# Attention scores: the low part of the keys in both partition halves, the third product over all rows, the value products of a step in one run, four prepared blocks

## The chip, the core and the metric

One NeuronCore of a Trainium2 chip runs the whole kernel. The metric is the device time in microseconds (us); the kernel before was run three times. The engines are TensorE (PE; its weight loads are listed apart as PEld), VectorE (DVE), ScalarE (ACT), GpSimd (POOL) and the DMA queue of SyncE (SP).

## What is computed

```python
def _attn_ref(q, k, v, w1, b1, w2):          # B 2, H 8, S 576, D 64
    scores = scale * np.matmul(q, k.transpose(0, 1, 3, 2))
    rel = (pos[:, None] - pos[None, :]).astype(np.float32)
    psi_rel = np.log1p(np.abs(rel))
    psi_i = np.log1p(np.maximum(pos[:, None].astype(np.float32), 1.0))
    x = (psi_rel / psi_i)[..., None]
    bias = np.maximum(x @ w1 + b1, 0.0) @ w2
    scores = scores + bias.transpose(2, 0, 1)[None, :, :, :]
    scores = scores - np.max(scores, axis=-1, keepdims=True)
    attn = np.exp(scores)
    attn = attn / (np.sum(attn, axis=-1, keepdims=True) + 1e-09)
    return np.matmul(attn, v)

def reference(...):
    x = attention output as 1152 rows of 512
    x = _moe_ref(x, ...)      # eight experts, 512 -> 1024 -> 512, with balanced weights P
    return _moe2_ref(x, ...)  # 512 -> 2048 -> 512 with an ELU between
```

## The kernel before

The program has an attention stage (to about 214 us) and, behind it, the expert and feed-forward stage with the products of lines 530 and 717, whose order a planner (`Plan.order`) makes at build time. The change lies in the attention stage, which is ordered by hand: every engine works off its instructions in the order in which the program issues them.

**Blocks and steps.** A block is a pair of heads `hp` and a batch `b`; there are eight. A step is one block and one query tile `t` of 128 rows (64 for `t` = 4): 40 steps. The first four blocks are interleaved (steps 0 to 19, the 64-row tile first), blocks 4 and 5 fill steps 20 to 29, blocks 6 and 7 steps 30 to 39; in these the two 64-row steps come last (28, 29 and 38, 39).

**Precision in two parts.** `load_qk` loads each block's queries and keys, transposed, twice: 64 head dimensions in partitions 0 to 63 and again in 64 to 127. `prep` (line 1152) casts both to fp32r on VectorE (`qs`, `kh`, line 1159), then subtracts on GpSimd: `qs` becomes the high part in one partition half and the low part in the other (line 1164), and `kl` the low part of the keys (line 1165). It is a generator of four pieces: cast, cast, subtractions of head 0, subtractions of head 1. `emit_qk` (line 1184) multiplies: over all 128 rows, (high + low query) times high key (line 1198), four products, two heads by two halves of the keys; then over the 64 rows of the high query, high query times low key (line 1203), four products, two of which can stand side by side in the array, as they use different rows. `QB` is the number of prepared blocks that have room at once.

**A step.** `run_step(s)` goes through the letters of `ORD_A` while bias groups are left (steps 0 to about 12), and of `ORD_B` after that. R, S: score plus bias and minimum of head 0, 1 on VectorE (`emit_ttr`). T, U: transposes of the previous step's exponentials, copied out by ScalarE (T) and VectorE (U). V: the last transpose, copied by ScalarE. N: reciprocal of the sums on VectorE and its broadcast on GpSimd (line 1239). E, F: exponentials on ScalarE. a: one of five pieces of the value products of two steps back (lines 1282, 1285; the fifth piece ends with the transpose of the broadcast reciprocal, line 1295). X: their result is taken out. Q: score products of the next step. p: one piece of `prep`, then two pieces of the background list `bg`. M, O, H, L: the bias network and its loads.

`PS` lists [block, step]: before that step the block's `prep` is put into the queue that p works off. `w_split` (steps 27 and 28) puts six entries into `bg`: four sums on GpSimd (line 302), four times a high part on ScalarE and a low part on VectorE (lines 315, 316), and a load; the third and fourth part need the sums. `ops_first` (steps 35 and 37) does the like for the first operands of the next stage (lines 332, 352, 353).

```python
    for i, s0 in PS:
        if s == s0:
            prep_q.append(prep(i))
    run_step(s)
    ...
    if s == 27:
        w_split()
    if s == 28:
        w_split()
```

## Time and profile before

| | |
|---|---|
| median of 3 runs | 1208.87 us (1208.53 to 1208.88) |
| the profiled execution's own time | 1207.91 us |
| its span, first to last instruction | 1206.1 us |
| PE busy | 1170.9 us, 97% of the span |
| DVE, ACT, POOL busy | 916.1, 626.4, 92.9 us |
| mean granted PE clock | 0.995 |

Busy shares are averages over stages with different limits, and matmuls overlap, so a busy PE is not a PE at its peak. The chain of waits says what released each piece of work; where it stays on PE, PE itself sets the pace. The rows come from one execution; its span and what lies around it make its time. In rows of products and transposes the first operand shape is rows by columns of the array.

### The profile page before, as it was taken

How to read it: one execution, taken by the hardware profiler on the slowest of the kernel's cores; microseconds unless marked ns; L12 is line 12 of the kernel's file. 1: busy time of each engine (PE TensorE's matmuls, PEld its weight loads, DVE VectorE, ACT ScalarE, POOL GpSimd, SP SyncE). 2: the span in 40 equal slices, each digit the busy share in tenths (PEclk: the TensorE clock that was granted, in tenths of full speed). 3: DMA queues.
4: the chain of work that ended last, by engine and by line, in shares of the span. 5: the costliest groups of instructions: out<-in, count | busy, mean ns of one | idle time of the engine just before them, and what ended most of it. 6: DMA issues, size and time to landing. Idle time of an engine off the chain costs nothing.

```text
span 1206.1 us, 19661 instructions
## 1 busy us (share of the span) xinstructions
PE 1170.9 (97%) x7432; PEld 986.9 (82%) x7432; DVE 916.1 (76%) x1932; ACT 626.4 (52%) x1413; POOL 92.9 (8%) x107
## 2 busy tenths in 40 slices
PE   7899999999999999999999999999999988999998
PEld 3467777788888888888888888888888876788887
DVE  8987787664587778778788787787776468788875
ACT  6797667554333444443434444444434346777763
POOL 4402453000000000000000000000000001000000
PEclk9999999899999999999999999999999999999999
DMA  8767741111112233242232323232411101111102
GB/s 227 221 213 200 208 122 35 33 56 53 36 36 79 80 88 102 67 129 76 92 106 88 105 87 104 90 100 68 130 45 53 53 1 36 53 53 36 36 1 79
DMA packets 36285, 104.78 MB, mean 87 GB/s; under 512 B 4064, under 2 KB 4192, under 8 KB 36192
## 3 DMA queue, kind: packets, MB, share of 16 engines
q1 hardware_dynamic: 36192, 103.54, 28.5%
q8 instruction: 58, 0.95, 0.3%
q14 instruction: 35, 0.29, 0.1%
HBM read 81.88 MB, written 21.64 MB: 86 GB/s over the span
## 4 chain that ended last, share of the span: by engine, by line
PE 91%; DVE 3%; ACT 1%; POOL 1%; issue 0%; DMA 0%; ACTq 0%; DVEq 0%
PE y L717 41%; PE m L530 38%; PE av L1285 3%; PE tr L1254 2%; PE bps L1406 2%; PE sc L1198 1%; PE sc L1203 1%; PE av L1295 1%; PE trl L1266 1%; PE av L1282 1%; PE lg L873 0%; DVE ol L353 0%; DVE et L1213 0%; DVE w1l L316 0%; DVE ol L430 0%
## 5 line engine op out<-in xcount | busy, mean ns | idle before, releaser
L530 PE MATMUL m<-oh,w1h 128*128 128x256 f32 (+1 forms) x1120 | 335.8, 300 | 3.8 <-DVE c L562 1.4
L530 PE MATMUL m<-oh,w1l 128*128 128x256 f32 (+1 forms) x1120 | 330.6, 295 | 3.8 <-ACT u L543 1.6
L530 PE MATMUL m<-ol,w1h 128*128 128x256 f32 (+1 forms) x1120 | 330.3, 295 | 2.6 <-DVE c L562 1.3
L717 PE MATMUL y<-w2h,hh 128*128 128x512 f32 x720 | 284.6, 395 | 2.9 <-ACT hh L637 1.5
L717 PE MATMUL y<-w2h,hl 128*128 128x512 f32 x720 | 283.4, 394 | 0.0
L717 PE MATMUL y<-w2l,hh 128*128 128x512 f32 x720 | 282.5, 392 | 0.8 <-DVE w2l L430 0.8
L530 PEld LDWEIGHTS m<-oh,w1h 128*128 128x128 f32 x1120 | 211.0, 188 | 45.8 <-ACT u L543 13.3
L530 PEld LDWEIGHTS m<-ol,w1h 128*128 128x128 f32 x1120 | 211.4, 189 | 22.4 <-DVE c L562 1.9
L530 PEld LDWEIGHTS m<-oh,w1l 128*128 128x128 f32 x1120 | 211.3, 189 | 5.6 <-ACT u L543 2.3
L717 PEld LDWEIGHTS y<-w2h,hh 128*128 128x128 f32 x720 | 135.1, 188 | 18.8 <-ACT hh L637 2.3
L717 PEld LDWEIGHTS y<-w2h,hl 128*128 128x128 f32 x720 | 135.1, 188 | 17.8
L543 ACT ACTIVATE p<-m 128x256 f32<-128x256 f32 (+1 forms) x160 | 65.8, 411 | 161.3 <-PE m L530 157.3
L717 PEld LDWEIGHTS y<-w2l,hh 128*128 128x128 f32 x720 | 135.2, 188 | 16.2 <-DVE w2l L430 1.4
L543 ACT ACTIVATE u<-m 128x256 f32<-128x256 f32 (+1 forms) x160 | 65.9, 412 | 132.0 <-PE m L530 128.7
L593 ACT ACTIVATE hh<-c 128x512 fp32r<-128x512 f32 (+3 forms) x128 | 72.1, 563 | 109.7 <-DVE c L562 109.6
L748 DVE SCALAR_TENSOR_TENSOR acc<-y,P,acc 128x512 f32<-128x512 f32 x126 | 94.5, 750 | 37.3 <-PE y L717 35.4
L596 DVE SCALAR_TENSOR_TENSOR hl<-c,hh 128x512 fp32r<-128x512 f32 (+3 forms) x128 | 77.5, 605 | 20.4 <-ACT hh L593 18.6
L562 DVE TENSOR_TENSOR c<-m,u 128x256 f32<-128x256 f32 (+1 forms) x80 | 36.6, 458 | 73.7 <-PE m L530 72.0
L1213 DVE CUSTOM_DVE_ANT_0 et<-sc,bt 128x576 f32<-128x576 f32 (+1 forms) x80 | 57.9, 751 | 22.0 <-PE sc L1203 17.3
L332 POOL TENSOR_TENSOR st<-xt,st 128x256 f32<-128x256 f32 (+1 forms) x8 | 6.7, 835 | 755.2 <-DVE st L332 755.0
L1228 ACT ACTIVATE et<-et,nmx 128x576 f32<-128x576 f32 (+1 forms) x80 | 61.3, 771 | 3.2 <-DVE nmx L1213 3.1
L423 ACT ACTIVATE w2h<-raw 128x512 fp32r<-128x512 f32 x80 | 48.6, 625 | 21.7 <-PE y L717 12.4
(136 smaller groups left out, 1600.1 us busy)
## 6 DMA issues: line engine op xcount, KB each, us to landing
raw<-w1p SPq DMA_DIRECT2D x32, 512.0 KB, 3.6
raw<-w2p SPq DMA_DIRECT2D x32, 512.0 KB, 3.6
scr<-o SPq DMA_DIRECT2D x36, 295.5 KB, 3.5
bt<-scr SPq DMA_DIRECT2D x16, 576.0 KB, 4.9
cw<-w1d SPq DMA_DIRECT2D x16, 512.0 KB, 4.4
wsc<-ca SPq DMA_DIRECT2D x32, 256.0 KB, 4.4
cw<-w2d SPq DMA_DIRECT2D x16, 512.0 KB, 4.4
raw<-wsc SPq DMA_DIRECT2D x16, 512.0 KB, 3.6
```

The costliest lines, as they stand in the source:

```text
L423: act.activation(out=dst(bh.get()), in_=src(), func=ACTF.Copy)
L530: lambda e, w=w, o=o, j=j, k=k: pe.matmul(x["ap"](bank), w.get()[:, ai, j, :], o.get()[:, bi, j, :], start=(k == 0 and i in (1, 2, 5)), st ...
L543: lambda e: act.activation(out=b.get()[:, 0:N], in_=x["ap"](bank), func=ACTF.Copy),
L562: lambda e: eng[e].tensor_tensor(out=blk(b.get()[:, half * N:half * N + N], rev), in0=ap(p), in1=ap(q), op=ALU.add),
L593: op([("A", cA(w))], lambda e: act.activation(out=hh(), in_=ap(), func=ACTF.Relu), r=sk, w=wh, after=gate_)
L596: lambda e: dve.scalar_tensor_tensor(out=bl.get()[:, d], in0=ap(), scalar=0.0, in1=hhf(), op0=ALU.max, op1=ALU.subtract),
L717: lambda e, a=a, w=w, f=f, i=i, y=y, c=c: pe.matmul(y.get(), a.get()[:, c], w.get(), start=(f == 0 and i == 0), stop=(f == 3 and i == 2)),
L748: lambda e: dve.scalar_tensor_tensor(out=a.get(), in0=y.get(), scalar=P[0][:, n, e_:e_ + 1], in1=a.get(), op0=ALU.mult, op1=ALU.add),
L1213: dve.tensor_tensor_reduce(out=e.rearrange("p (x j) -> p x j", x=2), in0=sc[0:r, :, 0:HALF], in1=biast[hp, t][0:r, h].rearrange("p (x j) - ...
L1228: act.activation(out=e, in_=e, func=ACTF.Exp, scale=-1.0, bias=nmx[0:r, h:h + 1], accum_out=sm[0:r, h:h + 1])
L1254: pe.transpose(p[:, 128 * j:128 * j + r], et[0:r, c0:c0 + 128], ident[0:r, 0:r])
L1285: pe.matmul(p[64 * h:64 * h + 64, 0:r], vt[:, j - 1, 64 * h:64 * h + 64], a[:, 4 * h + j - 1, 0:r], start=False, stop=(j == 4), skip_group ...
```

## The change

The low part of the keys, `kl`, is made for both heads in both partition halves (twice the room; each of its subtractions covers 128 partitions instead of 64). The low-key products then run over all 128 rows with the same weights as the first ones, (high + low query) times low key, and each head's four products follow each other. The fifth value piece moves from behind Q to the others, so that the five run as one. `QB` falls from 5 to 4, and `PS` moves four blocks to later steps.

```diff
--- before.py
+++ after.py
@@ -30,7 +30,7 @@
 NB = 2
 LAG = 1
 TO = [4, 0, 1, 2, 3]
-QB = 5
+QB = 4
 AB = 2
 BD = 1
 PRE = 12
@@ -39,9 +39,9 @@
 LV = [1, 2, 3, 4, 20, 19, 32, 28]
 ACC = [2.6, 3.1]
 WARM = 8
-PS = [[3, 0], [4, 12], [5, 16], [6, 19], [7, 25]]
+PS = [[3, 0], [4, 16], [5, 17], [6, 20], [7, 27]]
 ORD_A = "RXTSMOHUapaEaaNpFaLMOVQH"
-ORD_B = "RTSNUXaafLEafappFVQa"
+ORD_B = "RTSNUXaafLEafaappFVQ"
 TOFF = [0, 128, 256, 384, 512]
 TROW = [128, 128, 128, 128, 64]
 NN = [256, 320]
@@ -1152,7 +1152,7 @@
         def prep(i):
             qs = qkp.tile([128, 2, S], F32R, tag="qs", name="qs")
             kh = qkp.tile([128, 2, S], F32R, tag="kh", name="kh")
-            kl = qkp.tile([128, S], F32R, tag="kl", name="kl")
+            kl = qkp.tile([128, 2, S], F32R, tag="kl", name="kl")
             prepped[blocks[i]] = qs, kh, kl
             qr, kr = loaded.pop(i)
             for dst, src in ((qs, qr), (kh, kr)):
@@ -1160,9 +1160,9 @@
                 load["d"] += 0.73
                 yield
             for h in range(2):
-                o, u = slice(64 - 64 * h, 128 - 64 * h), slice(64 * h, 64 * h + 64)
+                o = slice(64 - 64 * h, 128 - 64 * h)
                 pool.tensor_tensor(out=qs[o, h], in0=qr[o, h], in1=qs.bitcast(F32)[o, h], op=ALU.subtract)
-                pool.tensor_tensor(out=kl[u], in0=kr[u, h], in1=kh.bitcast(F32)[u, h], op=ALU.subtract)
+                pool.tensor_tensor(out=kl[:, h], in0=kr[:, h], in1=kh.bitcast(F32)[:, h], op=ALU.subtract)
                 yield
 
         def prep_next():
@@ -1193,14 +1193,10 @@
             sc = [psA("sc") for _ in range(2)]
             qc = slice(TOFF[t], TOFF[t] + r)
             for h in range(2):
-                for x in range(2):
-                    kc = slice(HALF * x, HALF * x + HALF)
-                    pe.matmul(sc[h][0:r, x, 0:HALF], qs[:, h, qc], kh[:, h, kc], start=True, stop=False)
-            for x in range(2):
-                for h in range(2):
-                    kc = slice(HALF * x, HALF * x + HALF)
-                    hs = slice(64 * h, 64 * h + 64)
-                    pe.matmul(sc[h][0:r, x, 0:HALF], qs[hs, h, qc], kl[hs, kc], start=False, stop=True)
+                for w, last in ((kh, False), (kl, True)):
+                    for x in range(2):
+                        kc = slice(HALF * x, HALF * x + HALF)
+                        pe.matmul(sc[h][0:r, x, 0:HALF], qs[:, h, qc], w[:, h, kc], start=not last, stop=last)
             for h in range(2):
                 scs[s, h] = sc[h]
```

## Rows read from the trace of the kernel before

**Rows 1.** The page's chain that ended last, by engine, whole program
```profile
PE 91%; DVE 3%; ACT 1%; POOL 1%; issue 0%; DMA 0%; ACTq 0%; DVEq 0%
```

**Rows 2.** Chain of waits, one ordinary step (start, us, what)
```profile
127.18 0.26 PE trl L1266
127.44 0.54 PE sc L1198 x4
127.97 0.46 PE sc L1203 x3
128.43 0.37 PE av L1285 x4
128.80 0.26 PE av L1295
129.06 0.87 PE tr L1254 x8
129.94 0.22 PE av L1282 x2
130.16 0.81 PE av L1285 x12
```

**Rows 3.** Chain of waits in the steps with bias work
```profile
47.78 2.34 POOL qs L1164
...
101.32 0.59 PE tr L1254 x4
...
103.81 1.02 PE av L1285 x16
```

**Rows 4.** Timeline of VectorE, casts and reductions (start, us, instructions)
```profile
121.74 0.75 DVE L1213 CUSTOM_DVE_ANT_0 et<-sc,bt 128x576 f32<-128x576 f32 x1
...
131.27 0.75 DVE L1159 CAST qs<-ring 128x1152 fp32r<-128x1152 f32 x1
...
132.61 0.75 DVE L1213 CUSTOM_DVE_ANT_0 et<-sc,bt 128x576 f32<-128x576 f32 x1
```

**Rows 5.** Timeline of GpSimd, steps 17, 28 and 29
```profile
124.47 1.42 POOL L1164 TENSOR_TENSOR qs<-ring,qs 64x576 fp32r<-64x576 f32 x1
...
128.86 1.42 POOL L1165 TENSOR_TENSOR kl<-ring,kh 64x576 fp32r<-64x576 f32 x1
...
164.77 0.74 POOL L302 TENSOR_TENSOR st<-raw 128x256 f32<-128x256 f32 x1
165.59 0.73 POOL L302 TENSOR_TENSOR st<-st,raw 128x256 f32<-128x256 f32 x1
...
171.77 1.11 POOL L302 TENSOR_TENSOR st<-raw 128x256 f32<-128x256 f32 x1 [0.74 <-DVE w1l L316]
```

**Rows 6.** Timeline of TensorE, transposes of steps 28, 29 and 31
```profile
162.92 1.04 PE L1254 MATMUL tr<-csb,et 128*128 128x128 f32 x8
...
167.96 0.46 PE L1254 MATMUL tr<-csb,et 64*128 64x64 f32 x4 [0.76 <-ACT aT L1267]
...
176.94 0.66 PE L1254 MATMUL tr<-csb,et 128*128 128x128 f32 x4 [0.77 <-ACT aT L1267]
```

**Rows 7.** Timeline of ScalarE, a part of the second weight split
```profile
175.39 0.63 ACT L315 ACTIVATE w1h<-st 128x512 fp32r<-128x512 f32 x1 [0.69 <-POOL st L302]
```

**Rows 8.** Groups of GpSimd by form, the reciprocal's broadcast
```profile
L1239 POOL TENSOR_TENSOR rcb<-ones,rc 128x128 f32<-128x128 f32 x32 | 13.4, 421 | 92.9 <-DVE rc L1237 73.7 <-PE bps L1406 5.0 <-PE av L1295 4.6
...
L1239 POOL TENSOR_TENSOR rcb<-ones,rc 64x128 f32<-64x128 f32 x8 | 3.7, 464 | 21.0 <-DVE rc L1237 16.7 <-PE bps L1406 3.7 <-PE av L1285 0.5
```

**Rows 9.** Sums by window: span, engines' busy time, PEclk, DMA share, GB/s
```profile
33.10:36.50 3.40, 1.20 (x9) 0.18 (x6) 3.40 (x10) 2.29 (x6) 2.85 (x2) 1.00 0.94 231
36.52:39.93 3.41, 3.41 (x14) 1.23 (x14) 1.93 (x5) 1.02 (x3) 0.00 (x0) 0.50 0.73 263
```

**Rows 10.** Chain of waits behind step 36
```profile
197.89 2.04 DVE ol L353 x2
199.93 0.67 DVE et L1213
```

## What the change will do to the time

> **What bounds the kernel now.** I read the page first, for the chain that ended last: 91% of the span on TensorE (PE) [rows 1]. The change touches only the attention stage (to about 214 us), so I then read the chain of waits there, step by step. In the twenty-odd steps after the bias work has run out (steps 13 to 39, ordered by ORD_B), an ordinary step is eight pieces of PE work that add up to 3.79 us with no wait between them [rows 2]; 3.79 is also the distance from one step to the next. So here a saved PE microsecond is a saved microsecond, until another engine comes last. That happens in three places: at step 3 (Pool's subtractions), in steps 29 and 31, and from step 36 on. At steps 29 and 31 PE waits for the head-1 transposes (line 1254): the exponential of head 1 stands on ScalarE behind the third piece of a weight split, and that piece waits for Pool's sums [rows 6, 7]. From step 36 VectorE's low parts (line 353) run straight into the score reduction [rows 10].
>
> **The score products and the value run (PE).** Removed: the row-split products, .46 us with the change into that form, and the value run of four behind them, .37. Added: four full-row products at the price of the first four (.54/4 = .135 each), .54. Merged: the runs of 12 and 4 cost .81 + .37 = 1.18 [rows 2]; the run of 16 in the earlier steps costs 1.02 [rows 3]. The single transpose that now follows another full-array piece instead of a split one costs an eighth of .87, .11, instead of .26. New step: .87 + .22 + 1.02 + .26 + .11 + 8 x .135 = 3.56. It saves .23. The dearer bound for the four products is their present piece plus the same again for the lost pairing; the cheaper is .46 unchanged; I take .135 since it is the same shape, stream and tile form.
>
> The row shows .46 for four paired products, hardly less than .54 for four full ones. The Trainium skill, "TensorE: Matmul & The Clock Gate", Part 3 on packing small matmuls, says products on different row groups run side by side, which speaks against this change: two pairs would cost two products, .27, and the change would add .27 a step. "TensorEngine Tiling (Array Packing)", Key Properties, says that changing the tiling form drains the engine, which speaks for it. The trace agrees with both: pairs overlap, but the change of form eats most of it.
>
> In steps 4 to 12 (ORD_A) the value run is whole already. There only the products change: +.08 for them, and the four transposes behind them fall from .59 [rows 3] to half of .87, -.155 [rows 2]. That is -.075 each for eight steps, -.6. In the first four steps the query tile has 64 rows and there is little to win behind the products; with a tenth lost there I take -.5 for the stage, between 0 and -.8. Score head 0 is ready after four products instead of seven, head 1 after eight; VectorE starts at nearly the same place, which is off the path, so nothing.
>
> **The preparation (line 1152).** Two casts on VectorE, four subtractions on Pool, two a step. One subtraction of 64 x 576 takes 1.42, four in a row 5.8 (124.47 to 130.28) [rows 5]. Over 128 partitions instead of 64 the kl subtraction might cost more. Pool's broadcast takes .42 on 128 partitions and .46 on 64 [rows 8], so partitions do not count. The dearer bound is the line through .42 at 128 elements and .73 at 256 [rows 5, 8], which gives 1.5 at 576; the cheaper is 1.42, which I take.
>
> With four buffers block 4 can be cast only after step 15, and the list PS moves the others later: block 5 from steps 16 and 17 to 18 and 19; block 7 from 25 and 26 to 27 and 28. Block 6 (20, 21) keeps its distance. This is what costs.
>
> *Block 5.* Its four subtractions are issued in step 19, and the scores of step 21 need them at the end of step 20. Pool works in order and has the broadcast of that step (line 1239) ahead, which waits for the reciprocal, which stands behind the two reductions, which stand behind the casts. From the first reduction to the first subtraction it was 2.73 us (121.74 to 124.47) [rows 4, 5]. Casts start 2.2 after the transposes (131.27 against 129.06) and the next reduction 3.55 after them [rows 2, 4], which with a step of 3.56 is the very start of step 19. So the subtractions run from 2.4 to 2.7 after it to 8.2 to 8.5. The seventh product of those scores (head 1, kl) is due at 3.56 + 2.48 + .81 = 6.85. PE waits 1.5 us (1.0 to 1.9); nothing is behind it that could hide that. Before, block 5 had three steps to spare, so no wait.
>
> *Block 7.* In step 28 the first weight split is also fed: ORD_B calls the preparation, then two background pieces, at each p. Pool's queue was broadcast, four sums; it becomes broadcast, two subtractions, four sums, two subtractions, broadcast, and in step 29 the second four sums. Counted from the transposes of step 28 (162.92) [rows 6]: subtractions start at 2.6 and take 2 x 1.46 (to 5.5), the first two sums 1.55 (164.77 to 166.32) to 7.1, and from there to the released transposes it is 1.64 as before (to 167.96): 8.7 instead of 5.04 [rows 5, 6]. Going on in Pool's queue: all four sums 3.6 (to 9.1), two subtractions (12.1), broadcast (12.5), four sums 3.62 as from 171.77 to 175.39 (16.1), then 1.55 to the transposes of step 31 (176.94): 17.7 instead of 14.02 [rows 5 to 7]. The second contains the first. It costs 3.6 (2.9 to 4.2), and the savings of steps 28 to 30 are swallowed in it. Queued behind the waiting piece on ScalarE are the exponential of head 1 and the copy that frees the transposes' bank; PE waits for that copy.
>
> **Late steps.** Steps 31 to 35 save 4.5 x .23 = 1.0. From step 36 the chain runs through VectorE at its own pace: what PE saves there it waits for [rows 10]; about .1 is left in the tail.
>
> **Sum**, against the profiled execution of 1207.91 (span 1206.1): -.5 - 15 x .23 (steps 13 to 27) + 1.5 + 3.6 - 1.0 - .1 = +.05. That execution is 1 us below the median of the runs, 1208.87; the sum carries over, 1208.9. A measurement of this kernel can tell about .2%, 2.4 us, from no change.
>
> **Rivals.**
> *Gains survive* (25%). If Pool gets to the subtractions as soon as the casts are done, not behind the broadcast, they start 2.4 earlier: the 1.5 is gone and the 3.6 shrinks to 1.2, sum -3.9, 1205.0; with no pile-up at all -5.1, and -6 with the larger early saving, 1203. For it: the casts are done before the step begins, so the order alone holds Pool. Against: the subtraction did start right behind the broadcast [rows 5], and N stands ahead of p in both orders.
> *Pool slowed by VectorE* (22%), slower. A subtraction took 2.34 instead of 1.42 at 47.78 [rows 3], and sums of one shape took .73 and 1.11 [rows 5]. In step 28 Pool's longer queue runs beside VectorE's low parts of the same split. Two to four of its entries at the dearer price add 1.8 to 3.6: 1211 to 1212.5. It decides once the excess of the queue passes the 2.4 us margin of the measurement, i.e. from three such entries on; below that it lies in my own range.
> *The change of form stays* (5%), slower. If only .27 of the split products' .46 is theirs (two pairs at the price of two products) and the .19 left is paid in any case by the next change of form, a step of ORD_B saves .04, not .23: 19.5 steps lose 3.7, the nine of ORD_A 1.7, and the time is 1214.3. Against it: changes of form are fewer after it, and the transposes behind a split run cost .59 where those in a whole run of eight cost .435 [rows 2, 3]. This is what the rule on packing above would give.
> A fall of PE's clock is part of my range, not a rival: after a stretch in which PE was busy 1.20 of 3.40 us the granted clock was .50, the 1.2 GHz level, for 3.41 us [rows 9]. The wait at step 29 could do the same; but PE has 6.1 us of work up to the transposes of step 31 (8.7 to 14.8), due at 17.7, so the 1.7 us that one such stretch costs is hidden there, and .6 of two.
>
> **Numbers.** Forecast (within 1206.5 to 1211.3, no change) 48%; faster than that 25%; slower 27%. The likeliest one's own range is 1207 to 1211; to hold 8 in 10 it reaches to 1203.8 on the side of the surviving gains and 1212.7 on that of the slowed Pool.
>
> **What would show it.** Right: ordinary steps 3.55 apart; a wait of PE for Pool's kl at about the 21st step's scores; a gap of some 4 us before the head-1 transposes of step 29, released by ScalarE behind Pool's sums; the end of attention within 2 us of 214. Wrong: no such gap (Pool's order is not what I think), or ordinary steps still at 3.7 (the change of form was not the cost), or subtractions at twice their price.

## The result and the profile after

Six runs of the changed kernel took 1216.30 us in the median (1214.64 to 1220.36), six of the kernel before on the same chip 1208.45 (1205.47 to 1208.88): 1.0075 times the time, 95% interval 1.0056 to 1.0093. The profiled execution of the changed kernel took 1215.84, its span 1214.0, 7.8 us more than the span of before. The prediction was 1208.9, range 1203.8 to 1212.7: the change is slower, and outside the range.

The chain of waits of the changed kernel, one ordinary step (start, us, what), answers to [rows 2]:

```profile
141.94 1.07 PE sc L1199 x8
143.01 0.87 PE tr L1250 x8
143.88 0.22 PE av L1278 x2
144.10 1.02 PE av L1281 x16
145.13 0.26 PE av L1291
145.39 0.11 PE trl L1262
```

They add up to 3.55 us; before it was 3.79. So the saving is there, to the hundredth, and it is lost somewhere else. Five of the waits of the changed kernel from 104 to 185 us (who waited for whom, us in total, times, longest) name the places:

```profile
DVE et L1209 <- DMA bt<-scr: 5.3, 2, 2.7
...
ACT w1h L315 <- POOL st L302: 4.2, 1, 4.2
...
PE av L1291 <- POOL rcb L1235: 1.5, 1, 1.5
...
PE sc L1199 <- POOL kl L1165: 1.4, 1, 1.4
PE sc L1199 <- POOL qs L1164: 1.2, 1, 1.2
```

The starts of the first score product of each step, laid side by side, cut the loss into stretches. Here and below, "step 19" as a length is the distance from the first score product of step 19 to that of step 20.

| stretch | before | after | difference | predicted |
|---|---|---|---|---|
| steps 0 to 12 | 73.32 | 71.80 | -1.5 | -.5 |
| steps 13 to 18 | 22.23 | 22.85 | +.6 | -1.4 |
| step 19 | 3.79 | 5.12 | +1.3 | -.2 |
| step 21 | 3.79 | 6.72 | +2.9 | +1.3 |
| steps 20, 22 to 27 | 26.51 | 24.88 | -1.6 | -1.6 |
| steps 28 to 31 | 17.01 | 21.80 | +4.8 | +3.6 |
| steps 32 to 35 | 15.14 | 14.22 | -.9 | -1.0 |
| step 36 to the first product of line 530 | 20.63 | 21.81 | +1.2 | -.1 |
| from there to the end | 992.09 | 993.11 | +1.0 | 0 |

**Steps 13 to 18.** VectorE's timeline of the changed kernel (start, us, instructions, in brackets the idle time before and who ended it):

```profile
117.51 0.76 DVE L1209 CUSTOM_DVE_ANT_0 et<-sc,bt 128x576 f32<-128x576 f32 x1 [2.69 <-DMA bt<-scr]
```

and the same view of the kernel before:

```profile
117.91 0.76 DVE L1213 CUSTOM_DVE_ANT_0 et<-sc,bt 128x576 f32<-128x576 f32 x1 [1.60 <-DMA bt<-scr]
```

A load of bias tiles lands at about the same time in both. Before, VectorE waited 1.60 for it and PE none; in the changed kernel VectorE is there earlier and waits 2.69, and the rest reaches PE: steps 15 to 18 take 3.85, 3.92, 4.14 and 3.83, 1.5 us over four steps of 3.55. The shorter steps are only a part of the cause. VectorE's 1.5 us of lead (it stood ready at 114.82 instead of 116.31) are the lead of steps 0 to 12, as steps 13 to 15 took 10.95 against 10.88. And the load took longer: from its issue to VectorE's start 11.6 us (105.96 to 117.51), before 10.2 (107.70 to 117.91); the load of tiles ahead of it 6.5 (102.90 to 109.44), before 5.7 (104.42 to 110.09). In e7_hold, whose program is the changed kernel's up to step 28, they took 9.9 (105.80 to 115.66) and 5.3 (102.74 to 108.02), and steps 15 to 18 took 14.2, with no loss. VectorE's timeline of that run:

```profile
115.66 0.76 DVE L1209 CUSTOM_DVE_ANT_0 et<-sc,bt 128x576 f32<-128x576 f32 x1 [1.57 <-DMA bt<-scr]
```

With steps of 3.79, e2_ps lost .95 where the later load took 11.6, and e12_hold .2 where it took 10.8; e17_sumsfirst, with steps of 3.55, lost .8 at 10.8. By these executions an estimated .6 of the 1.5 come from the shorter steps and the rest from the loads.

**Steps 19 and 21.** PE's timeline, the three products at which it stood:

```profile
131.23 0.33 PE L1291 MATMUL av<-csb,rcb 128*128 128x128 f32 x1 [1.51 <-POOL rcb L1235]
...
136.97 0.53 PE L1199 MATMUL sc<-kh,qs 128*128 128x288 f32 x2 [1.22 <-POOL qs L1164]
...
138.91 0.54 PE L1199 MATMUL sc<-kl,qs 128*128 128x288 f32 x2 [1.42 <-POOL kl L1165]
```

GpSimd's timeline in the same stretch answers to [rows 5]:

```profile
126.97 1.94 POOL L1164 TENSOR_TENSOR qs<-ring,qs 64x576 fp32r<-64x576 f32 x1
128.88 1.94 POOL L1165 TENSOR_TENSOR kl<-ring,kh 128x576 fp32r<-128x576 f32 x1
130.77 0.40 POOL L1235 TENSOR_TENSOR rcb<-ones,rc 128x128 f32<-128x128 f32 x1
...
132.09 1.43 POOL L1164 TENSOR_TENSOR qs<-ring,qs 64x576 fp32r<-64x576 f32 x1
133.60 1.45 POOL L1165 TENSOR_TENSOR kl<-ring,kh 128x576 fp32r<-128x576 f32 x1
135.00 1.92 POOL L1164 TENSOR_TENSOR qs<-ring,qs 64x576 fp32r<-64x576 f32 x1
136.88 1.98 POOL L1165 TENSOR_TENSOR kl<-ring,kh 128x576 fp32r<-128x576 f32 x1
```

and VectorE's casts beside it:

```profile
134.72 0.94 DVE L1159 CAST qs<-ring 128x1152 fp32r<-128x1152 f32 x1
135.59 1.99 DVE L1159 CAST kh<-ring 128x1152 fp32r<-128x1152 f32 x1
```

At 130.77 the broadcast that PE waits for in step 19 comes out from behind block 4's subtractions, the last two of which took 1.94 each beside block 5's casts. The four subtractions of block 5 follow from 132.09. Two of them run alone, 1.43 and 1.45; two run beside block 6's casts, 1.92 and 1.98, and the casts take .94 and 1.99 instead of .75.

**Steps 28 to 31.** PE's timeline, the head-1 transposes of step 29 (they answer to the second line of [rows 6]):

```profile
173.03 0.69 PE L1250 MATMUL tr<-csb,et 64*128 64x64 f32 x4 [4.77 <-ACT aT L1263]
```

GpSimd's timeline up to it:

```profile
166.50 1.43 POOL L1164 TENSOR_TENSOR qs<-ring,qs 64x576 fp32r<-64x576 f32 x1
168.01 1.73 POOL L1165 TENSOR_TENSOR kl<-ring,kh 128x576 fp32r<-128x576 f32 x1
169.70 0.90 POOL L302 TENSOR_TENSOR st<-raw 128x256 f32<-128x256 f32 x1
170.68 0.72 POOL L302 TENSOR_TENSOR st<-st,raw 128x256 f32<-128x256 f32 x1
```

and ScalarE's:

```profile
171.43 0.63 ACT L315 ACTIVATE w1h<-st 128x512 fp32r<-128x512 f32 x1 [4.23 <-POOL st L302]
171.97 0.76 ACT L1224 ACTIVATE et<-et,nmx 64x576 f32<-64x576 f32 x1
...
172.72 0.25 ACT L1263 ACTIVATE aT<-trl 128x128 f32<-128x128 f32 x1
```

The three timelines, read back from PE, are as the prediction has it: transposes behind the copy of the last transpose, that behind the exponential of head 1, that behind a piece of the weight split, that behind GpSimd's sums, these behind two subtractions. And two stretches at half clock, by windows (after the stretch: its length, busy time and instructions of PE, PEld, VectorE, ScalarE and GpSimd, PEclk, DMA share, GB/s):

```profile
171.90:178.70 6.80, 5.67 (x31) 4.66 (x32) 6.14 (x12) 4.40 (x13) 5.70 (x7) 0.50 0.55 161
...
216.30:226.50 10.20, 9.66 (x63) 8.42 (x64) 4.38 (x14) 2.59 (x10) 0.39 (x1) 0.50 0.00 0
```

The first begins within PE's wait of 4.77, the second behind waits of .55 and 1.02. The kernel before had one at 36.52 [rows 9] and one at 214.0 for 6.8 us.

### The profile page after: what moved, and what is told of

It is laid out like the page before. It is cut to its first block, busy times and chain, and to the rows that moved or that the text cites. A ratio compares the mean times of both kernels' runs of the same rounds, so it can differ in the third digit from the quotient of the medians.

```text
span 1214.0 us, 19669 instructions
## 1 busy us (share of the span) xinstructions
PE 1169.4 (96%) x7432; PEld 1002.1 (83%) x7432; DVE 919.6 (76%) x1932; ACT 626.2 (52%) x1413; POOL 93.7 (8%) x107
## 4 chain that ended last, share of the span: by engine, by line
PE 88%; DVE 4%; POOL 2%; ACT 1%; issue 1%; DMA 1%; DVEq 0%; POOLq 0%; ACTq 0%
PE y L717 41%; PE m L530 38%; PE sc L1199 2%; PE av L1281 2%; PE tr L1250 2%; PE bps L1402 1%; DMA bt<-scr 1%; DVE et L1209 1%; POOL qs L1164 1%; POOL kl L1165 1%; PE av L1278 1%; PE av L1291 0%; PE lg L873 0%; DVE ol L353 0%; ACT et L1224 0%
```

## The experiments

All were timed against the kernel before on the same chip. Their numbers first, in one table (us; "tail" is from the first score product of step 39 to the first product of line 530, "rest" from there to the end; from one profiled execution each, the ratios from all runs):

| kernel | ratio, 95% interval | ordinary step | step 19 | step 21 | steps 29 to 31 | tail | rest |
|---|---|---|---|---|---|---|---|
| before | 1 | 3.79 | 3.79 | 3.79 | 13.28 | 8.83 | 992.1 |
| after | 1.0075 [1.0056, 1.0093] | 3.55 | 5.12 | 6.72 | 18.25 | 10.15 | 993.1 |
| e2_ps | 1.0096 [1.0071, 1.0121] | 3.79 | 3.79 | 8.20 | 20.99 | 10.26 | 992.2 |
| e6_oldord | 1.0075 [1.0047, 1.0103] | 3.86 | 3.86 | 8.72 | 18.23 | 8.68 | 991.1 |
| e1_ord | .9995 [.9976, 1.0013] | 3.62 | 4.35 | 3.62 | 12.85 | 8.91 | 994.0 |
| e8_six | .9984 [.9963, 1.0005] | 3.63 | 3.63 | 3.62 | 17.75 | 9.14 | 993.6 |
| e9_b6 | 1.0069 [1.0054, 1.0084] | 3.55 | 5.13 | 5.66 | 20.86 | 9.22 | 993.2 |
| e10_b6lq | 1.0052 [1.0036, 1.0067] | 3.55 | 5.13 | 7.24 | 18.42 | 10.14 | 993.7 |
| e4_b7 | 1.0015 [.9996, 1.0034] | 3.55 | 5.13 | 8.23 | 13.99 | 10.08 | 993.5 |
| e17_sumsfirst | 1.0063 [1.0037, 1.0089] | 3.56 | 5.08 | 8.26 | 18.18 | 9.43 | 992.7 |
| e16_afterpp | 1.0077 [1.0055, 1.0100] | 3.55 | 5.12 | 8.03 | 18.77 | 10.81 | 991.1 |
| e7_hold | 1.0039 [1.0020, 1.0058] | 3.55 | 4.98 | 8.16 | 17.72 | 8.82 | 991.1 |
| e12_hold | .9972 [.9958, .9986] | 3.79 | 3.79 | 3.79 | 13.28 | 9.06 | 990.4 |
| e11_sixhold | .9951 [.9929, .9973] | 3.63 | 3.63 | 3.63 | 14.15 | 8.88 | 990.4 |
| e15_less | .9943 [.9925, .9961] | 3.62 | 3.62 | 3.63 | 12.71 | 8.87 | 989.4 |
| e13_pp | 1.0003 [.9982, 1.0024] | 3.63 | 3.63 | 3.65 | 14.63 | 10.85 | 989.3 |
| e14_best | .9986 [.9972, 1.0000] | 3.56 | 3.66 | 6.10 | 14.03 | 8.88 | 989.3 |

### Which part costs: the places, the order, the products

The theory from the profile: the new places of the preparations cost more than the whole loss, and the products and the order give a part of it back. First the places alone, on the kernel before (e2_ps):

```diff
-QB = 5
+QB = 4
-PS = [[3, 0], [4, 12], [5, 16], [6, 19], [7, 25]]
+PS = [[3, 0], [4, 16], [5, 17], [6, 20], [7, 27]]
```

> The kernel before with QB 4 and the new PS alone; products and order as before. Theory P: PE waits for the low keys at the scores of step 21 (1.5 to 3 us) and for Pool's sums at step 29 (3.5 more than before), perhaps with a fall of PE's clock, and the time is 1213 to 1218. Theory O: 1210 or less.

Ratio 1.0096, more than was expected, though by the intervals not to be told from the changed kernel's 1.0075. The step stays at 3.79, and the waits of steps 21 and 29 are there without a new product. PE's timeline of this run:

```profile
136.36 0.53 PE L1198 MATMUL sc<-kh,qs 128*128 128x288 f32 x2 [1.15 <-POOL qs L1164]
...
138.28 0.74 PE L1203 MATMUL sc<-kl,qs 64*128 64x288 f32 x3 [1.05 <-POOL kl L1165]
```

So these two waits come from the places (and the four buffers behind them), not from the 128-partition subtraction (kl is cut to 64 here) nor from shorter steps.

The order alone, on the kernel before (e1_ord), and the changed kernel with the old order (e6_oldord):

```diff
-ORD_B = "RTSNUXaafLEafappFVQa"
+ORD_B = "RTSNUXaafLEafaappFVQ"
```

> The kernel before with the new ORD_B alone (the five value pieces in one run); products, buffers and PS as before. Theory P (the later place of the preparation makes the change slow): an ordinary step falls from 3.79 to about 3.63 (1.02 for the run of 16 in place of 1.18), no wait at steps 19 to 21 or a longer one at step 29, and the time is 1205.5 to 1208. Theory O (the new order or the new products themselves cost): 1210 or more.

> The changed kernel with the old ORD_B (the fifth value piece behind Q). Against e2_ps it shows the full-row products alone, against the changed kernel the merged value run alone. Theory P: 1216 to 1219, a little slower than the changed kernel, since the steps grow by about .2 where nothing else comes last. Theory O, with the order at fault: 1210 to 1213.

With the split products the new order saves .16 a step (3.63). With full products and the old order the step is 3.86, .07 dearer than before; with both it is 3.55. So the full-row products cost .07 beside the old order and save .08 beside the new one. The chains of waits show why, first e6_oldord, one step:

```profile
145.84 0.81 PE av L1281 x12
146.65 0.26 PE trl L1262
146.91 1.06 PE sc L1199 x8
147.96 0.37 PE av L1281 x4
148.33 0.26 PE av L1291
148.59 0.87 PE tr L1250 x8
```

Against [rows 2] only the score products have changed, 1.06 instead of 1.00. Then e1_ord:

```profile
123.05 0.26 PE av L1295
123.31 0.11 PE trl L1266
...
124.56 1.06 PE tr L1254 x8
```

Here the split products run straight into the transposes, which take 1.06 instead of .87. A piece that follows one of another form (128*64 value products, 64*128 split score products) is .15 to .19 dearer: a single transpose .26 instead of .11, eight .87 or 1.06. Full products save only where they take such a change away. In the old order there is none to take: the single transpose ahead of them has their form, and value products, which have another form either way, stand behind them.

The wait of step 19 belongs to the order: PE's timeline of e1_ord,

```profile
131.15 0.33 PE L1295 MATMUL av<-csb,rcb 128*128 128x128 f32 x1 [0.65 <-POOL rcb L1239]
```

and with the old order it is gone (e6_oldord, step 19 at 3.86, no gap). The single transpose of the reciprocal comes half a step earlier in the merged run, while GpSimd still has the subtractions of a block ahead of the broadcast. e1_ord reaches line 530 2.5 us earlier than the kernel before in their profiled executions, but its runs can't be told from those of before.

### Step 19: the transpose out of the run

The kernel before with the value products in one run and the transpose as a sixth piece (e8_six); in ORD_B it stands behind Q, in ORD_A it follows the fifth piece at once, as before:

```diff
-                    else:
+                    elif j < 5:
...
-                    if j == 4:
+                    if j == 5:
...
-            return [piece(j) for j in range(5)]
+            return [piece(j) for j in range(6)]
-ORD_A = "RXTSMOHUapaEaaNpFaLMOVQH"
-ORD_B = "RTSNUXaafLEafappFVQa"
+ORD_A = "RXTSMOHUapaEaaNpFaaLMOVQH"
+ORD_B = "RTSNUXaafLEafaappFVQa"
```

> The kernel before with the value products of a step in one run as in the new order, but the transpose of the broadcast reciprocal made a sixth piece that stays behind the scores, where PE took it before; buffers, PS and products as before. Theory R (in e1_ord PE waits at step 19 because the run brings that transpose forward by half a step, ahead of Pool's broadcast): ordinary steps 3.63, no wait for the broadcast at step 19, 1205 to 1207.5. Its rival (the broadcast is late anyway): the wait of .9 stays and the time is that of e1_ord, 1207 to 1209.

Step 19 takes 3.63, with no wait: the place of the one transpose was the cause. The gain of the shorter steps is then lost again at step 29, where PE now waits 1.81 for the head-1 transposes and the clock falls; windows of this run:

```profile
166.90:180.60 13.70, 13.56 (x82) 10.88 (x84) 9.34 (x28) 8.13 (x23) 4.90 (x8) 0.50 0.43 145
```

Ratio .9984, within what can't be told from no change.

### Step 21: casts and subtractions in each other's way

The changed kernel with block 6's preparation three steps later (e9_b6), so that block 5's subtractions have no casts beside them:

```diff
-PS = [[3, 0], [4, 16], [5, 17], [6, 20], [7, 27]]
+PS = [[3, 0], [4, 16], [5, 17], [6, 23], [7, 27]]
```

> The changed kernel with block 6 prepared from step 23 instead of 20. Theory S (casts on VectorE and subtractions on Pool slow each other where they run together): block 5's last two subtractions fall from 1.9 to about 1.45, the second cast of step 20 from 1.98 is gone, and PE's wait for them at the scores of step 21 falls from 3.2 to about 2; the wait at step 19 stays; 1213.5 to 1215.5. Theory W (subtractions over 128 partitions are slow by themselves): the last two stay at 1.9 and the time at 1215 to 1217.

GpSimd's timeline, the last two subtractions of block 5:

```profile
135.76 1.43 POOL L1164 TENSOR_TENSOR qs<-ring,qs 64x576 fp32r<-64x576 f32 x1
137.16 1.41 POOL L1165 TENSOR_TENSOR kl<-ring,kh 128x576 fp32r<-128x576 f32 x1
```

They are back at their price alone, and step 21 takes 5.66 instead of 6.72: the other 2.1 us over 3.55 is the late start, the 1.1 is the mutual slowing. Block 4's subtractions still run beside block 5's casts (1.93 and 1.96), and step 19 stays at 5.13. The run as a whole is no faster (1.0069): bias tiles landed .8 us later and PE's clock fell for 13.7 us at 172.5 instead of 6.8. With block 6's queries and keys also loaded three steps later (e10_b6lq):

```diff
-LQ = [4, 11, 105, 114, 116, 121]
+LQ = [4, 11, 105, 114, 119, 121]
```

> As e9_b6, and block 6's queries and keys are loaded in step 19 instead of 16, behind the next bias tiles in SP's queue. Theory D (the bias tile of steps 16 and 17, which shares the transfers with those loads, sets the pace there): it lands about 5 us earlier than at 117.4, steps 15 and 16 run at 3.55 and the scores of step 19 come 1 us earlier than in e9_b6. Its rival (PE, VectorE or Pool set the pace there): the tile lands earlier and steps 15 to 18 stay at 3.8 to 4.1.

The reduction that waits for the bias tile starts at 116.32 instead of 118.27 in e9_b6, 2 us earlier and not the 5 of theory D, and steps 15 to 18 together take 14.5 us (16.2 without this edit, 15.7 in the changed kernel). That fits loads of queries and keys ahead of the bias tiles, but it isn't shown: e4_b7, below, takes 14.7 for the same steps without the edit, so the landing differs by this much from one execution to the next. Ratio 1.0052; step 21 took 7.24 in this run, with a fall of the clock at 137.5 in it. It took 8.2 to 8.3 in e4_b7, e7_hold and e17_sumsfirst, which have the changed kernel's program up to there, each with a fall of 3.4 us at 137 to 138: of these four executions the changed kernel's own, with 6.72, is the one without a fall there.

### Steps 28 to 31: which queue

Block 7's preparation back at step 25, all else as changed (e4_b7):

```diff
-PS = [[3, 0], [4, 16], [5, 17], [6, 20], [7, 27]]
+PS = [[3, 0], [4, 16], [5, 17], [6, 20], [7, 25]]
```

> The changed kernel with block 7 prepared from step 25 again, as the kernel before has it (its buffer is free there too). Theory P: the pile in Pool's queue at step 28 is gone, the gap before the transposes of step 29 falls from 5.0 to about 1 us, PE's clock does not fall there, and the time is 1209 to 1212. Theory O: it stays at 1215 to 1217.

Ratio 1.0015 instead of 1.0075: some 7 us (by the intervals 4 to 10) hang on this one entry. Steps 29 to 31 take 13.99 instead of 18.25.

That says where, not which queue. In the next run (e17_sumsfirst) only the order within GpSimd's queue changes: the background entries come ahead of the preparation's piece.

```diff
-                    prep_next()
-                    do_bg(2)
+                    do_bg(2)
+                    prep_next()
```

> The changed kernel with one swap: in each background slot the two background entries come ahead of the preparation's piece, so that in step 28 GpSimd has broadcast, four sums, four subtractions in its queue instead of broadcast, two subtractions, four sums, two subtractions. Theory (GpSimd's queue sets both waits, and the second contains the first): head-1 transposes of step 29 about 5.0 us after the transposes of step 28, as before (wait .8 instead of 4.77, step 29 takes 5 to 6), but the head-1 transposes of step 31 still 17.7 to 18.6 after them, since the same entries are ahead of the second split's sums; first score product of step 32 at 183.4 to 184.3 instead of 184.82; ratio to before 1.005 to 1.0075. Rival 1 (the second wait was the first one passed on): the first score product of step 32 at 181 or earlier, ratio 1.004. Rival 2 (the casts and low parts on VectorE hold it, not GpSimd's queue): step 29 still over 9.

PE's timeline, the head-1 transposes of steps 29 and 31; the transposes of step 28 began at 164.80:

```profile
170.53 0.46 PE L1250 MATMUL tr<-csb,et 64*128 64x64 f32 x4 [1.63 <-ACT aT L1263]
...
182.55 1.11 PE L1250 MATMUL tr<-csb,et 128*128 128x128 f32 x4 [0.91 <-ACT aT L1263]
```

5.73 us behind step 28's transposes instead of 8.87, since the sums come first; but step 31's come 17.75 behind them, where the prediction's walk through the whole queue gave 17.7. Step 29 is 4.5 us shorter and nothing is won: 18.18 instead of 18.25 for the three steps. (The clock was down from 172.2 to 189.3 in this execution, and steps 32 to 35 took 16.01 instead of 14.22; PE still had to wait at step 31.) The second wait did contain the first. The wait of step 29 is still 1.63, where .8 was expected: two of the four sums took 1.06 and 1.17 in this run instead of .73, beside VectorE's low parts.

Then ScalarE's place (e16_afterpp): the changed kernel with the two background pieces behind the exponential and the copy they stood ahead of.

```diff
-ORD_B = "RTSNUXaafLEafaappFVQ"
+ORD_B = "RTSNUXaafLEafaaFVppQ"
```

> The changed kernel with the two background pieces of a step moved behind the second exponential and the copy of the last transpose on ScalarE (its letters pp behind F and V instead of ahead), nothing else. Theory A (as in the prediction: PE waits in step 29 for the exponential of head 1, which stands on ScalarE behind the split piece that waits for GpSimd's sums): that exponential is now ahead of it, the wait of 4.77 us falls under 1, step 29 takes 4.5 to 6 instead of 10.42, the wait moves to step 31 and the first score product of step 32 comes at 182.5 to 184. Theory B (the piece moved stands then ahead of the copy of the next step's transposes, on ScalarE, and its low part ahead of the other copy, on VectorE; any place behind GpSimd's sums stops PE a few pieces later): step 29 and 30 together still take 13 to 14.3 us, the first score product of step 32 at 184.3 to 185.5.

PE's timeline:

```profile
173.50 0.27 PE L1262 MATMUL trl<-csb,et 64*128 64x64 f32 x1 [2.25 <-ACT aT L1254]
175.15 0.53 PE L1199 MATMUL sc<-kh,qs 128*128 128x288 f32 x2 [1.38 <-DVE nmx L1209]
...
177.77 1.09 PE L1250 MATMUL tr<-csb,et 64*128 64x64 f32 x8 [0.61 <-DVE aT L1256]
```

No wait is left before the head-1 transposes, and three others stand in its place; steps 29 to 31 take 18.77. The piece that waits for GpSimd now stands ahead of the next step's copies on ScalarE and VectorE. Theory B holds (steps 29 and 30 take 13.25 together), though the first score product of step 32 came at 186.38, later than either theory had it: the piece that waits for GpSimd's queue stops whatever comes next on its own engine.

The same move in the kernel with the sixth piece (e13_pp, against e11_sixhold below) was a miss as a test of step 29: the 3.3 us of useless products there covered the wait either way.

```diff
-ORD_B = "RTSNUXaafLEafaappFVQa"
+ORD_B = "RTSNUXaafLEafaaFVppQa"
```

> As the kernel with the sixth piece and the useless products, but with the two background pieces of a step behind the second exponential and the copy of the last transpose on ScalarE, not ahead of them. Theory (the exponential of head 1 stands on ScalarE behind a weight-split piece that waits for GpSimd): the wait of PE in step 29 is under .5 us, that step takes about 4.5 us plus the 1.5 us of useless products, 5.3 to 6, and the first score product of step 32 comes at 177 to 178. Rival 1 (GpSimd's queue itself holds the step, through the broadcast of the reciprocal): step 29 still 7. Rival 2 (the time comes back where the split's parts are read): step 29 falls, the first product of line 530 doesn't come earlier than in the kernel without this move.

Both take 7.11 for step 29. But the move costs later: PE's timeline has a new wait,

```profile
178.73 1.21 PE L1198 MATMUL sc<-kh,qs 128*128 128x288 f32 x4 [0.69 <-DVE nmx L1213]
```

and the tail takes 10.85 instead of 8.88, so rival 2 of its expectation has it, though step 29 doesn't fall; ratio 1.0003 against .9951.

### The clock: what a fall costs

Useless products ahead of the head-1 transposes keep PE busy through a wait. In the changed kernel, 20 in step 29 and 5 in step 40 (e7_hold):

```diff
+        def hold(s, n):
+            if n:
+                w = psC[s % 2]("warm")
+                for _ in range(n):
+                    pe.matmul(w[:, 0:128], ones, ones, start=True, stop=True)
...
                 elif x == "U" and tr:
+                    hold(s, {29: 20, 40: 5}.get(s, 0))
                     emit_tr(d, 1)
```

> The changed kernel with products of no use in two gaps of PE, 20 before the head-1 transposes of step 29 and 5 before those of step 40, whose result nobody reads. Theory C (falls of PE's clock cost part of the loss): the clock stays up through steps 29 and 30, the score products of step 30 end about 2.9 us earlier against those of step 29, the transposes of step 31 about 1 earlier (Pool's queue comes next), the fall at the end of attention goes or shrinks and gives 2 to 3 more; 1211 to 1213.5. Theory N (the clock is no term): 1215 to 1217.

Ratio 1.0039 instead of 1.0075, some 4 us (by the intervals 1 to 8). PE's timeline:

```profile
172.65 0.46 PE L1250 MATMUL tr<-csb,et 64*128 64x64 f32 x4 [0.15 <-ACT aT L1263]
...
182.21 0.66 PE L1250 MATMUL tr<-csb,et 128*128 128x128 f32 x4 [1.93 <-ACT aT L1263]
```

The clock stays up at 172, step 29 is 1.6 shorter, and most of that is waited for at step 31: steps 29 to 31 win .5. At the end no later wait takes the gain back: the tail takes 8.82 instead of 10.15 and the rest 991.1 instead of 993.1, together 3.4 us.

The kernel before alone, 4 in step 29 and 5 in step 40 (e12_hold; the same edit with `{29: 4, 40: 5}`):

> The kernel before, unchanged but for useless products ahead of the head-1 transposes: 4 in step 29 and 5 in step 40 (no output changes). It prices the clock fall at the end of the attention stage in the kernel before (214.0, 6.8 us). Theory (the fall is paid for): first product of line 530 at about 213, no fall at 214, from there to the end about 990.5 instead of 992.1; median 1205.5 to 1206.5, ratio .9975 to .9985. Rival (what follows waits for loads or VectorE anyway): same time within .1%, ratio .999 to 1.001.

Ratio .9972, 3.4 us. It has no fall at 214; rest 990.4 instead of 992.1, tail 9.06 instead of 8.83. So a part of what before spends is such a fall too: 1.4 us of it show in these two profiles, and where the rest of the 3.4 comes from stays open. The kernel with the sixth piece and 14 in step 29 (e11_sixhold), then 6 (e15_less):

> The kernel before with its row-split low-key products and its preparation list, with the value products in one run and the transposed reciprocal as a sixth piece behind the score products, and 14 useless products ahead of the head-1 transposes of step 29 (1.5 us of a wait of 2.0 there) and 5 in step 40; they change no output. Theory (a fall of the clock behind a wait of PE is paid for): no fall of 13.7 us at 167, steps 30 and 31 take about 4 us each instead of 5.45 and 5.12, first score product of step 32 at 178 to 179 instead of 181.2, no fall at 214, first product of line 530 at 212 to 213 instead of 215.9; median about 1203.5, ratio to before .995 to .997. Rival (PE isn't the limit there, ScalarE's queue is): the fall goes and the time stays, 1207, ratio .9985.

> The kernel before with the value products in one run, the transposed reciprocal as a sixth piece, and useless products ahead of the head-1 transposes: 6 in step 29 instead of 14, and 5 in step 40 (no output changes). Each of them turned out as two instructions of .118 us, so 14 took 3.32 us where the wait was 2.0; 6 take 1.42. Theory (14 were more than the wait, the clock needs only a part of it filled): step 29 takes about 5.9 instead of 7.11, first score product of step 32 at 176.6 to 177.9 instead of 177.85, since the sums of the second split are next there; no fall of the clock at 167; median 1201.5 to 1202.5, ratio .994 to .9955. Rival (a wait of .6 us left open is enough for a fall): a fall of 3 to 14 us near 167, first score product of step 32 at 179 to 181, ratio .996 to .998.

Ratios .9951 and .9943, the best of all; the two can't be told apart by their runs. Windows of e15_less, the stretch that ran at .50 in e8_six:

```profile
166.90:180.60 13.70, 13.29 (x139) 10.57 (x139) 12.00 (x37) 11.35 (x33) 6.52 (x9) 1.00 0.56 188
```

Filled to .3 us, the wait brings no fall in this execution. I had sized the 14 wrongly: each product shows as two instructions of .118 us, so they took 3.3 us for a wait of 1.8, and steps 29 to 31 took 14.15 against 12.71 with 6.

### The changed products in the best places

The changed kernel with block 6 at 23 and its loads three steps later, block 7 at 25, the transpose as a sixth piece, 14 useless products in step 29 and 5 in step 40 (e14_best):

```diff
-PS = [[3, 0], [4, 16], [5, 17], [6, 20], [7, 27]]
+PS = [[3, 0], [4, 16], [5, 17], [6, 23], [7, 25]]
-LQ = [4, 11, 105, 114, 116, 121]
+LQ = [4, 11, 105, 114, 119, 121]
```

> The changed kernel with its full-row low-key products and four buffers, with block 6's preparation at step 23 instead of 20 and its queries and keys loaded three steps later, block 7's at 25 instead of 27, the transposed reciprocal as a sixth piece, 14 useless products in step 29 and 5 in step 40. Theory (the places of the preparations, the early transpose and the two clock falls hold all of the loss): no wait in step 19 (3.65), step 21 still 6 to 8 us since block 5 is prepared late, step 29 at most 6.5, ordinary step 3.6, first score product of step 32 at 178 to 180, first product of line 530 at 213 to 215; median 1204 to 1206, ratio .996 to .998, level with the kernel before with the sixth piece and the useless products. Rival (four buffers cost more elsewhere): 1208 or above.

Ratio .9986, short of the .996 to .998 of the theory, against .9951 for the kernel with split products and the same useless products: full products come out some 4 us behind (by the intervals 1 to 7). They save .08 in an ordinary step, 2.2 us over steps 13 to 39 if nothing stood in the way, but with four prepared blocks block 5 was late in every place tried for the others: step 20 takes 4.19, step 21 6.10, and steps 26 and 27, now beside block 7's preparation, 4.03 each. The best kernel of the study is the one before with its split products, the transpose of the reciprocal as a sixth piece and a few useless products: about 7 us (5 to 9) faster than before.

## Why the prediction was wrong

**Right.** The ordinary step: 3.55 against 3.56, piece by piece (.87, .22, 1.02, .26, .11, 1.07 against .87, .22, 1.02, .26, .11, 1.08), and 1.6 us saved over steps 20 and 22 to 27. It holds only for order and products together: neither alone does what the sum of the two does (e6_oldord, e1_ord). In that the rival on the change of form had a point for the old order, where the products alone cost .07 a step, and none for the new one; that its time, 1214.3, comes near the measured one is luck, since it rests on a step that saves .04. The Trainium skill, "TensorEngine Tiling (Array Packing)", Key Properties, has it that a change of the tiling form drains the engine; the trace agrees, with .15 to .19 us for one. The price of the subtraction over 128 partitions is the cheaper bound, 1.43 and 1.45 alone. The wait of step 21 at the scores, the wait of step 29 (transposes 8.87 us behind those of step 28, predicted 8.7) and GpSimd's queue up to step 31 (17.75 in e17_sumsfirst, predicted 17.7) are where the prediction put them.

**Step 19, +1.3: not seen.** The change moves the transpose of the reciprocal with the fifth piece, and the prediction priced it on PE alone (.26, as before). It did not ask what the transpose reads. It comes half a step earlier, and the broadcast that it reads stands behind block 4's subtractions, which the change had also moved there. e1_ord, e6_oldord and e8_six show it from three sides. For the subtractions of blocks 5 and 7 the prediction did go back through GpSimd's queue; for this transpose, and for block 4's subtractions, it did not. By the prices alone (1.94 against 1.42 and 1.44), an estimated 1.0 of the wait of 1.51 is block 4's slowing beside block 5's casts.

**Steps 15 to 18, +1.5: put at nothing.** The load's wait stood in VectorE's timeline of before, 1.60 us, and cost nothing there, because PE had as much in hand. The prediction took -.23 a step here without asking what that cover was worth. But the shorter steps make only some .6 of the 1.5; the rest is a load that took 1.4 us longer than in the execution of before, and e7_hold loses nothing (steps 13 to 18 took 21.2 to 23.3 us in the kernels with full products and the new order).

**Step 21, +2.9 instead of +1.3: mis-sized.** The place and the mechanism were right, the price not. Four subtractions were counted at 1.42; two took 1.92 and 1.98. That VectorE slows GpSimd was a rival in the prediction, at 22%, but for step 28 and its sums; the row that showed it, 2.34 at 47.78 [rows 3], was not applied to the casts that the same list PS puts beside them. e9_b6 removes the casts and gets 1.1 us of it. The start was late too: the first subtraction, at 132.09, is 4.7 us behind the transposes that open the step (127.43) and not 2.4 to 2.7, since GpSimd had block 4's subtractions and two broadcasts to finish. Most of this is the wait of step 19, which PE had already paid; .6 is left, the 2.1 of e9_b6 against 1.5.

**Steps 28 to 31, +4.8 instead of +3.6: queue right, rest short.** The queue gave 8.87, and up to step 31 18.5 instead of 17.7 (182.21 in e7_hold, whose step 28 began its transposes at 163.74). Beside low parts a subtraction took 1.73, another 1.88 and a sum .90, some .9 us more than alone; a start of the subtractions at 2.3 instead of 2.6 takes .3 of it back. The fall of the clock was said to be hidden but for .6 us: e7_hold gives .5. So this term was about 1 us short, and for the reason that the rival named.

**The tail, +2.2 instead of -.1: a term put at nothing.** The prediction asked what a wait does to the clock at step 29 and not at the end of the stage, where before had its own fall at 214.0. With that wait filled in both kernels (e7_hold, e12_hold), the stretch from step 36 to the end takes 1011.5 and 1011.3 us, level as predicted; with falls of 10.2 and 6.8 us it takes 1014.9 and 1012.7. So by these profiles the fall costs 3.4 us in the changed kernel and 1.4 in the kernel before (3.4, from 1.7 to 5.1, by the runs of e12_hold). That the changed kernel's was the longer one is not shown to be the change's doing: e9_b6 and e17_sumsfirst, with the changed products and order there, had falls of 6.8 us, as before.

**Steps 0 to 12, -1.5 instead of -.5.** Most of it isn't the change: e12_hold, whose first steps are those of before, took 72.09 there with the same two falls of the clock, at 14 and 24. Against that the change saves .3. Of the eight steps that were to save .075 each, two do (steps 5 and 7); in the others PE isn't what sets the time.

The range failed because each wait was reckoned alone, at the prices of an undisturbed queue. The steps of the prediction that failed are two waits sized too small (step 21, 1.5 instead of 3.2; steps 28 to 31, 3.6 instead of 4.8) and three put at nothing (step 19, the load, the fall at the end). The first two are there in e2_ps with the old products and order, so they don't come from shorter pieces on PE; the third is the early transpose. The load and the fall at the end differ between executions of the same program, so their shares of the +7.8 us are this execution's, though the runs as a whole are as much slower; why the load took longer stays open.

## What to carry to other kernels

Before a saving on the engine that sets the pace is multiplied by the number of steps, read the idle time of every other engine in those steps: a wait of 1.6 us that costs nothing today lies under a cover, which shorter steps make thinner. When work is moved to another engine's busy steps, price it by a row in which both are busy (1.9 here), not by one in which it is alone (1.42). When an instruction is moved, follow its operands back through the queue that makes them, also for the smallest instruction of the move. And where a wait of PE can't be removed, a few useless products in it can be worth more than the change itself, but only where nothing else is late right behind it, and only as many as the wait is long.

## What the runs showed of the hardware

**VectorE's casts and GpSimd's subtractions take turns.** From 133.60 on the ends follow each other: kl 135.05, cast 135.66, qs 136.92, cast 137.58, kl 138.86, that is 1.45, .61, 1.26, .66 and 1.28 us apart: what each takes alone, or a little less, one after the other, while both show as busy. In e9_b6, without casts, the same subtractions take 1.43 and 1.41. The reductions of line 1209 beside them stay at .74 to .76. The Trainium skill, "SBUF — State Buffer", section "SBUF: two separate sides", has it that the two engines share a pair of ports and that one holds them for a whole instruction while the other stands; the trace agrees for these forms, to within .2 us.

**A wait of PE can be paid twice.** The granted clock was 1.00 or .50 in every stretch looked at (2.4 and 1.2 GHz), and the falls, 3.4 to 17.1 us long, lie behind waits of PE: 4.77 us in the changed kernel at step 29, 1.81 in e8_six. Not every wait brings one: 2.20 us in e1_ord at the same place did not. Whether one comes differs between executions of one kernel: the ten of e8_six had mean clocks of .985 to .990 and 1209.7 to 1211.5 us five times, of .994 to .997 and 1202.2 to 1204.7 us the other five. So a single profile says too little about a kernel with such a wait; with the wait filled to .3 us (e15_less) all ten lie between 1201.2 and 1204.8.
